# Row sums of the first half-batch by TensorE, and the weight rounding and the MLP's first block respaced, in a routed attention with an MLP behind it

## The chip, the cores and the metric

The kernel runs on one core of one Trainium2 chip. The metric is the device time of one execution in microseconds. The core's engines work side by side and wait for one another by semaphores: TensorE (PE in the profile; PEld is its weight load) does matrix products and transposes into PSUM, VectorE (DVE) and GpSimd (POOL) work element by element, ScalarE (ACT) does functions and copies, and SyncE (SP) issues the transfers. Each engine takes its instructions in the order of the program.

## What is computed

Attention over 4 batches, 8 heads, 768 positions and 64 dimensions, in which a query sees only the keys that have the same nearest centroid (16 per head), and then an MLP with a gated activation on the 3072 x 512 result. Cut from the reference:

```python
q_assign = np.argmax(np.einsum('bhsd,hcd->bhsc', q_n, c_n), axis=-1)
k_assign = np.argmax(np.einsum('bhsd,hcd->bhsc', k_n, c_n), axis=-1)
mask = q_assign[:, :, :, None] == k_assign[:, :, None, :]
scores = np.where(mask, scale * np.matmul(q, k.transpose(0, 1, 3, 2)), -1000000000.0)
attn = np.exp(scores - np.max(scores, axis=-1, keepdims=True))
attn = attn / (np.sum(attn, axis=-1, keepdims=True) + 1e-09)
x = np.matmul(attn, v)            # then (B,H,S,D) -> (B*S, H*D) = 3072 x 512
h = x @ w_in                      # 512 x 2048
g = h * (1.0 / (1.0 + np.exp(-1.702 * h)))
out = (g @ w_out).astype(np.float32)
```

The two weights come as 64-bit floats, and the kernel makes 32-bit ones of them itself.

## The kernel before

Heads go in pairs: 16 pairs (4 batches x 4), each in two halves of the queries, which gives 32 groups `g` of 6 units (one per 128 keys, `kt`). A batch is 8 groups: the first halves of its four pairs, then the second halves. A turn `t` handles two units, so a group takes TG = 3 turns, half a batch 12, a batch TB = 24, and the loop has 96 turns and two to finish. In the first batch (`p < HP`) the mask comes from a second matmul, `part`, added to the scores; later VectorE does it.

```python
xp = ctx.enter_context(tc.tile_pool(name="xp", bufs=HP + 2))    # HP = 4
ps_s = ... bufs=2; ps_o = ... bufs=1; ps_m = ... bufs=3          # PSUM; bank() takes of ps_m

def split_w(i):                     # first part of the rounding of weight chunk i of 32
    e = wp.tile([P, WN], I32, name="e")                          # wp: bufs=3, WN = 512
    nc.vector.tensor_scalar(out=e, in0=hi, ... bitwise_and)                       # L159
    nc.vector.tensor_scalar(out=w.bitcast(I32), in0=hi, ... bitwise_and)          # L161
    nc.scalar.activation(out=e, in_=e, func=AF.Relu, ...)                         # L163
    nc.scalar.activation(out=w, in_=w.bitcast(I32), func=AF.Copy, ...)            # L165

def join_w(i):
    nc.vector.scalar_tensor_tensor(out=e, in0=raw[:, :, 1], ..., in1=e, ...)      # L171
    nc.vector.scalar_tensor_tensor(out=w, in0=raw..., ..., in1=w, ...)            # L174
    nc.vector.tensor_tensor(out=w, in0=w, in1=e.bitcast(FP32), op=ALU.mult)       # L177

def round_next():                   # one round
    i = w_done[0]
    if i < NW:
        load_w(i + 2)
        split_w(i)
    if 0 < i <= NW:
        join_w(i - 1)
    w_done[0] += 1

def exps(u):                        # L409
    nc.scalar.activation(out=A_of[u] if p < HP else s, in_=s, func=AF.Exp, scale=SCALE)

def mask(u):
    ...                             # p >= HP: VectorE masks into A (L420)
    A = A_of[u]
    if kt == 0:
        return
    if kt == 1:
        sum_of[g] = ap.tile([P, 2, HALF], FP32, name="sum", bufs=2)
    nc.gpsimd.tensor_tensor(out=sum_of[g],                                        # L430
                            in0=A_of[u - 1] if kt == 1 else sum_of[g],
                            in1=A, op=ALU.add)

def values(u):
    for a in range(2):
        nc.tensor.matmul(out=o_of[g][a * D:(a + 1) * D, 0:HALF],                  # L441
                         lhsT=v_in[p][:, a, kt, :], rhs=A[:, a, :],
                         start=(kt == 0), stop=(kt == NJ - 1))
    ...                             # at kt == 5 ScalarE copies the result (L446)

def normalise(g):
    sm = sum_of.pop(g)
    ps = bank()
    for a in range(2):
        nc.tensor.matmul(out=ps[a * D:(a + 1) * D, 0:HALF], lhsT=ones,            # L453
                         rhs=sm[:, a, :], start=True, stop=True)
    rec = recs[g] = short()
    nc.vector.reciprocal(out=rec, in_=ps[:, 0:HALF])                              # L456
    nc.vector.tensor_tensor(out=x, in0=x, in1=rec, op=ALU.mult)                   # L458
    if g % HP == HP - 1:
        ffn.extend(ffn_chunks(g // HP))
```

`check` then has ScalarE test the reciprocals (L468, L470). The MLP of half a batch is 28 chunks: 16 `first(f)` (matmuls with `w_in`, L487; ScalarE's tanh, L492; VectorE's gate, L494) and 12 `second(n, part)` (matmuls with `w_out`, L504). Both begin with `round_to(...)`, which rounds the weights they need if that has not been done. Preparing a pair `p` takes seven steps `i`: transposes of q and k with a copy by ScalarE (0 to 3; L262, L267), products with the centroids (4, `prep_near`), the assignment by VectorE (5) and the spreading of the codes (6; in the first batch by transposes, L349, with copies by VectorE and ScalarE, L354, L356).

```python
rate = (NF + NH * (NF // 4)) / (TB / 2 - 0.5)
for t in range(NT + 2):
    ...                             # scores, part, exps of the turn's two units
    second = t >= TB // 2
    if second:
        round_next()
    ...                             # mask of the two units
    work = sorted(prep_at.get(t, ()), key=lambda w: PREP[w[1]] != prep_near)
    ...                             # prep_near steps; values of the turn before
    owed = owed + rate if ffn else 0.0
    g = (t - 2) // TG if t >= 2 and (t - 2) % TG == TG - 1 else None
    if g is not None and second:
        normalise(g)
    for p, i in work:
        prep(p, i)
    if g is not None and not second:
        normalise(g)
    if recs:
        check(*recs)
    if second or t and t % 4 != 3:
        round_next()
    while owed >= 1 and ffn:
        ffn.popleft()()
        owed -= 1
    if second and t % 2:
        round_next()
```

Of the kernel before, what the change touches and what calls it, by code (L numbers as in the profile page):

```python
# [10 lines left out]
I32 = mybir.dt.int32  # L11
# [27 lines left out]
def fast(  # L39
# [21 lines left out]
    nc = tc.nc  # L61

    B, H, S, D = q.shape
    NC = centroids.shape[1]
    DM, DF = moe_w_in.shape
    P = 128
    NJ = S // P
    HALF = S // 2
    NH = NJ // 2
    HP = H // 2  # L70
    NPAIR = B * HP
    NCH = DM // P
    NF = DF // P
# [10 lines left out]
    wp = ctx.enter_context(tc.tile_pool(name="wp", bufs=3))  # L84
    asg = ctx.enter_context(tc.tile_pool(name="asg", bufs=2))
    tmp = ctx.enter_context(tc.tile_pool(name="tmp", bufs=3))
    ap = ctx.enter_context(tc.tile_pool(name="ap", bufs=4))
    xp = ctx.enter_context(tc.tile_pool(name="xp", bufs=HP + 2))
    gp = ctx.enter_context(tc.tile_pool(name="gp", bufs=NF))
    yp = ctx.enter_context(tc.tile_pool(name="yp", bufs=2))  # L90
    dram = ctx.enter_context(tc.tile_pool(
        name="dram", bufs=2, space=bass.MemoryType.DRAM))
# [5 lines left out]
    def bank():  # L98
        return ps_m.tile([P, 512], FP32, name="m")
# [33 lines left out]
    WN = 512  # L133
# [6 lines left out]
    NW = len(w_chunks)  # L140
# [13 lines left out]
    def split_w(i):  # L154

        hi = w_raw[i][:, :, 1]
        w = w_chunks[i][0]
        e = wp.tile([P, WN], I32, name="e")
        nc.vector.tensor_scalar(out=e, in0=hi, scalar1=EXP, scalar2=None,  # L159
                                op0=ALU.bitwise_and)  # L160
        nc.vector.tensor_scalar(out=w.bitcast(I32), in0=hi, scalar1=0xFFFFF,  # L161
                                scalar2=None, op0=ALU.bitwise_and)
        nc.scalar.activation(out=e, in_=e, func=AF.Relu, scale=8.0,  # L163
                             bias=low[:, 0:1])
        nc.scalar.activation(out=w, in_=w.bitcast(I32), func=AF.Copy,  # L165
                             scale=2.0 ** -20, bias=1.0)
        w_pow[i] = e
# [12 lines left out]
    w_done = [0]  # L180

    def round_next():
# [4 lines that stand above are left out]
        if 0 < i <= NW:  # L187
            join_w(i - 1)
        w_done[0] += 1

    def round_to(n):
        while w_done[0] <= min(n, NW):
            round_next()

    load_qk(1, 0)
    load_v(0)
# [12 lines left out]
    ones = const.tile([P, D], FP32, name="ones")  # L209
# [34 lines left out]
    for a in range(2):  # L244
        rows = slice(a * D, (a + 1) * D)
        nc.vector.tensor_copy(
            out=cT[rows, :, a, :],
# [115 lines left out]
    PREP = [lambda p, i=i: prep_turn(p, i) for i in range(4)]  # L363
# [4 lines left out]

    NG = 2 * NPAIR
    NU = NG * NJ  # L370
    s_of, A_of, sum_of, o_of, O_of, xT_of = {}, {}, {}, {}, {}, {}

    def split(g):
        b, r = divmod(g, 2 * HP)
# [36 lines left out]

    def mask(u):

        g, kt = divmod(u, NJ)
        p, h = split(g)
        s = s_of.pop(u)
        if p >= HP:
            A_of[u] = ap.tile([P, 2, HALF], FP32, name="A")
            for a in range(2):
                nc.vector.scalar_tensor_tensor(  # L420
                    out=A_of[u][:, a, :],
                    in0=qcode[p][:, a, h * HALF:(h + 1) * HALF],
                    scalar=code[p][:, kt % NH, 1, kt // NH, a:a + 1],
                    in1=s[:, a, :], op0=ALU.is_equal, op1=ALU.mult)
        A = A_of[u]
        if kt == 0:
            return
        if kt == 1:
            sum_of[g] = ap.tile([P, 2, HALF], FP32, name="sum", bufs=2)
# [5 lines that stand above are left out]
        g, kt = divmod(u, NJ)  # L435
        p, h = split(g)
        if kt == 0:
            o_of[g] = ps_o.tile([P, 512], FP32, name="o")
        A = A_of.pop(u)
        for a in range(2):  # L440
            nc.tensor.matmul(out=o_of[g][a * D:(a + 1) * D, 0:HALF],  # L441
                             lhsT=v_in[p][:, a, kt, :], rhs=A[:, a, :],
                             start=(kt == 0), stop=(kt == NJ - 1))
        if kt == NJ - 1:
            O_of[g] = xp.tile([P, HALF], FP32, name="x")
            nc.scalar.copy(O_of[g], o_of.pop(g)[:, 0:HALF])  # L446

    def normalise(g):

        sm = sum_of.pop(g)  # L450
        ps = bank()
        for a in range(2):
            nc.tensor.matmul(out=ps[a * D:(a + 1) * D, 0:HALF], lhsT=ones,  # L453
                             rhs=sm[:, a, :], start=True, stop=True)
        rec = recs[g] = short()
        nc.vector.reciprocal(out=rec, in_=ps[:, 0:HALF])  # L456
        x = xT_of[g] = O_of.pop(g)
# [3 lines that stand above are left out]
# [11 lines left out]
                             accum_out=sums[:, 1, g:g + 1])  # L472


    ffn = deque()

    def ffn_chunks(bh):
        b, h = divmod(bh, 2)
        xT = [xT_of.pop(bh * HP + c) for c in range(NCH)]
        hs, ys = {}, {}  # L480

        def first(f):

            round_to((f * P // WN + 1) * NCH)
            ps = bank()
            for c in range(NCH):
                nc.tensor.matmul(out=ps[:, 0:HALF],  # L487
                                 lhsT=w_in[:, c, f * P:(f + 1) * P],
                                 rhs=xT[c], start=(c == 0),
                                 stop=(c == NCH - 1))  # L490
            g = hs[f] = gp.tile([P, HALF], FP32, name="g")
            nc.scalar.activation(out=g, in_=ps[:, 0:HALF], func=AF.Tanh,  # L492
                                 scale=0.851)
            nc.vector.scalar_tensor_tensor(out=g, in0=g, scalar=1.0,  # L494
                                           in1=ps[:, 0:HALF], op0=ALU.add,
                                           op1=ALU.mult)

        def second(n, part):
            round_to(NW // 2 + 4 * (part + 1))
            if part == 0:  # L500
                ys[n] = bank()
            ps = ys[n]
            for f in range(4 * part, 4 * part + 4):
                nc.tensor.matmul(out=ps[:, 0:DM],  # L504
                                 lhsT=hs[f][:, n * P:(n + 1) * P],
                                 rhs=w_out[:, f, :],
                                 start=(f == 0), stop=(f == NF - 1))
            if part == NF // 4 - 1:
                y = yp.tile([P, DM], FP32, name="y")
                nc.scalar.mul(y, ps[:, 0:DM], 0.5)  # L510
                nc.sync.dma_start(
                    out=out[b * S:(b + 1) * S, :].rearrange(
                        "(p j) n -> p j n", j=NJ)[:, h * NH + n, :], in_=y)

        return ([lambda f=f: first(f) for f in range(NF)]
                + [lambda n=n, part=part: second(n, part)
                   for n in range(NH) for part in range(NF // 4)])


# [25 lines left out]
        if i in (1, 3) and loads:  # L545
            load_qk(*loads.popleft())

    rate = (NF + NH * (NF // 4)) / (TB / 2 - 0.5)
    owed = 0.0
    for p, i in [(0, i) for i in range(6)] + [(1, i) for i in range(2)]:  # L550
        prep(p, i)
        if p == 0 and i in (1, 3):
# [1 line left out]
    for t in range(NT + 2):  # L554
        us = range(2 * t, 2 * t + 2) if t < NT else ()
        for u in us:
            scores(u)
        if t == 0:
            prep(0, 6)
        for u in us:  # L560
            part(u)
        for u in us:
            exps(u)
        second = t >= TB // 2
        if second:
            round_next()
        for u in us:
            mask(u)
        work = sorted(prep_at.get(t, ()), key=lambda w: PREP[w[1]] != prep_near)
        while work and PREP[work[0][1]] == prep_near:  # L570
            prep(*work.pop(0))
        if 1 <= t <= NT:
            for u in range(2 * t - 2, 2 * t):
                values(u)
        owed = owed + rate if ffn else 0.0
        g = (t - 2) // TG if t >= 2 and (t - 2) % TG == TG - 1 else None
        if g is not None and second:
            normalise(g)
        for p, i in work:
            prep(p, i)  # L580
        if g is not None and not second:
            normalise(g)
        if recs:
            check(*recs)
        if second or t and t % 4 != 3:
            round_next()
        while owed >= 1 and ffn:
            ffn.popleft()()
            owed -= 1
        if second and t % 2:  # L590
            round_next()
# [5 lines left out]
    ok1 = const.tile([P, 1], FP32, name="ok1")  # L597
    nc.vector.tensor_reduce(out=ok1, in_=ok, axis=AX.XY, op=ALU.min)
    for _ in range(NF // 2):
        ffn.popleft()()  # L600
    ps = bank()
    nc.tensor.transpose(out=ps[0:1, 0:P], in_=ok1, identity=ident)
    okt = const.tile([1, 1], FP32, name="okt")
# [2 lines left out]
    nc.vector.tensor_scalar(out=bad, in0=okt, scalar1=-1.0, scalar2=1.0,  # L606
                            op0=ALU.mult, op1=ALU.add)
    while ffn:
        ffn.popleft()()
        if len(ffn) == 4:  # L610
            is_bad = nc.values_load(bad[0:1, 0:1], min_val=0, max_val=1)
    return is_bad
# [440 lines left out]
```

## Time and profile before

| what | value |
|---|---|
| time, median of 3 runs | 1087.03 us (1086.46 to 1089.19) |
| span of the profiled run | 1087.3 us |
| TensorE busy | 1049.0 us, 96% |
| VectorE busy | 490.8 us, 45% |
| ScalarE busy | 354.8 us, 33% |
| GpSimd busy | 296.9 us, 27% (160 row-sum additions: 235.5 and 60.0 us) |
| mean granted TensorE clock | 0.99 |

Busy shares are means over a span with different stages; the windows by turn are needed to read them. A group of instructions is a line of the program with an engine and an operation: its count, its busy time, the mean duration of one in ns, and after the second bar the idle time of the engine just before them with what ended most of it. TensorE's records overlap one another, so its mean duration is longer than what a record adds to the time. In the timeline the brackets hold the engine's idle time before the row and what released it.

### The profile page before, as it was taken

What the parts mean: (1) busy time and instruction counts of PE and PEld (TensorE: products, weight loads), DVE (VectorE), ACT (ScalarE), POOL (GpSimd) and SP (SyncE); (2) the same over time, 40 slices, a digit from 0 to 9 for tenths busy, and PEclk for the clock granted to TensorE, in tenths of its full rate; (3) what the DMA queues carried; (4) which work ended last, traced back from release to release, by engine and by line L of the source; (5) the groups of instructions that cost most, each with busy time, mean ns of one, the idle gap of its engine ahead of it and who ended that gap; (6) DMA issues with size and microseconds to landing.
All of it is one profiled execution on the core that took longest, in us unless ns stands there. A gap on an engine that the chain in (4) does not pass through costs nothing. (4 is left out here: it accounts for less than half of the span.)

```text
span 1087.3 us, 10456 instructions
## 1 busy us (share of the span) xinstructions
PE 1049.0 (96%) x3982; PEld 492.6 (45%) x3982; DVE 490.8 (45%) x744; ACT 354.8 (33%) x665; POOL 296.9 (27%) x168
## 2 busy tenths in 40 slices
PE   7878799999999999999999999999999999999997
PEld 3423344445544455444454445444554445444543
DVE  3889999225442344424453164423552344431200
ACT  3755555223422333223432233223332133311100
POOL 2644223213232333123231142222332333230000
PEclk9998899999999999999999999999999999999999
DMA  7623443110100010002100000010000000000000
GB/s 199 165 81 116 131 133 111 46 49 17 49 23 27 10 30 15 31 25 54 51 23 17 15 20 15 15 48 32 8 7 12 10 10 1 1 10 20 1 11 22
DMA packets 64813, 45.13 MB, mean 42 GB/s; under 512 B 51953, under 2 KB 57585, under 8 KB 64753
## 3 DMA queue, kind: packets, MB, share of 16 engines
q1 hardware_dynamic: 64608, 44.33, 14.3%
q8 instruction: 33, 0.54, 0.2%
q14 instruction: 28, 0.22, 0.1%
q10 hardware_dynamic: 144, 0.03, 0.0%
HBM read 38.04 MB, written 6.31 MB: 41 GB/s over the span
## 5 line engine op out<-in xcount | busy, mean ns | idle before, releaser
L430 POOL TENSOR_TENSOR sum<-sum,A 128x768 f32<-128x768 f32 x128 | 235.5, 1840 | 461.3 <-DVE A L420 364.1
L487 PE MATMUL m<-x,w_in 128*128 128x384 f32 x1024 | 347.1, 494 | 9.7 <-ACT T L267 4.4
L504 PE MATMUL m<-w_out,g 128*128 128x512 f32 x768 | 337.8, 594 | 0.7 <-ACT short L282 0.7
L420 DVE SCALAR_TENSOR_TENSOR A<-qb,code,s 128x384 f32<-128x384 uint8 x288 | 157.6, 609 | 274.6 <-ACT s L409 251.9
L487 PEld LDWEIGHTS m<-x,w_in 128*128 128x128 f32 x1024 | 192.2, 192 | 149.1 <-issue 16.3
L504 PEld LDWEIGHTS m<-w_out,g 128*128 128x128 f32 x768 | 143.3, 190 | 175.6 <-issue 171.5
L494 DVE SCALAR_TENSOR_TENSOR g<-g,m 128x384 f32<-128x384 f32 x128 | 70.0, 553 | 220.4 <-ACT g L492 220.3
L384 PE MATMUL s<-T,T 64*128 64x384 f32 x768 | 152.9, 517 | 9.7 <-ACT A L409 9.6
L409 ACT ACTIVATE s<-s 128x768 f32<-128x768 f32 x144 | 107.9, 792 | 136.0 <-PE s L384 136.0
L441 PE MATMUL o<-A,inv 128*64 128x384 f32 x768 | 146.3, 502 | 0.0
L492 ACT ACTIVATE g<-m 128x384 f32<-128x384 f32 x128 | 61.7, 487 | 196.4 <-PE m L487 196.3
L430 POOL TENSOR_TENSOR sum<-A 128x768 f32<-128x768 f32 x32 | 60.0, 1876 | 215.6 <-DVE A L420 179.5
L384 PEld LDWEIGHTS s<-T,T 64*128 64x128 f32 x768 | 66.6, 189 | 94.6 <-issue 52.2
L456 DVE RECIPROCAL short<-m 128x384 f32<-128x384 f32 x32 | 81.6, 2551 | 25.8 <-PE m L453 25.8
L441 PEld LDWEIGHTS o<-A,inv 128*64 128x64 f32 x768 | 46.8, 137 | 84.8 <-issue 84.1
L510 ACT ACTIVATE y<-m 128x512 f32<-128x512 f32 x24 | 14.3, 595 | 155.8 <-PE m L504 142.7
L468 ACT ACTIVATE short<-short 128x384 f32<-128x384 f32 x32 | 16.7, 523 | 111.2 <-DVE x L458 111.2
L409 ACT ACTIVATE A<-s 128x768 f32<-128x768 f32 x48 | 36.1, 804 | 22.0 <-PE s L398 22.0
L267 ACT COPY T<-m 128x384 f32<-128x384 f32 x64 | 29.7, 480 | 37.2 <-PE m L262 37.1
L262 PE MATMUL m<-ident,in 128*128 128x128 f32 x192 | 33.9, 298 | 3.1 <-ACT T L267 1.7
L163 ACT ACTIVATE e<-e,low 128x512 int32<-128x512 int32 x32 | 23.1, 722 | 28.8 <-DVE e L159 28.8
L262 PEld LDWEIGHTS m<-ident,in 128*128 128x128 f32 x192 | 21.5, 146 | 22.4 <-issue 11.9
(68 smaller groups left out, 373.5 us busy)
## 6 DMA issues: line engine op xcount, KB each, us to landing
raw<-in_moe_w_in_dram SPq DMA_DIRECT2D x16, 512.0 KB
raw<-in_moe_w_out_dram SPq DMA_DIRECT2D x16, 512.0 KB
in<-in_q_dram SPq DMA_DIRECT2D x32, 192.0 KB
in<-in_k_dram SPq DMA_DIRECT2D x32, 192.0 KB
inv<-in_v_dram SPq DMA_DIRECT2D x16, 384.0 KB
out_dram<-y SPq DMA_DIRECT2D x24, 256.0 KB
qb<-line SPq DMA_DIRECT2D x12, 192.0 KB
line<-row SPq DMA_DIRECT2D x12, 1.5 KB
```

Of the source, the lines that this page charges most:

```text
L262: nc.tensor.transpose(out=ps[:, n * P:(n + 1) * P], in_=qk_in[p, w][:, h * NH + n].rearrange("p a d -> p (a d)"), identity=ident)
L267: nc.scalar.copy(dst, ps[:, 0:HALF])
L384: nc.tensor.matmul(out=ps[:, a, 0:HALF], lhsT=T[p, 1][rows, kt * P:(kt + 1) * P], rhs=T[p, 0][rows, h * HALF:(h + 1) * HALF], start=True, ...
L409: nc.scalar.activation(out=A_of[u] if p < HP else s, in_=s, func=AF.Exp, scale=SCALE)
L420: nc.vector.scalar_tensor_tensor(out=A_of[u][:, a, :], in0=qcode[p][:, a, h * HALF:(h + 1) * HALF], scalar=code[p][:, kt % NH, 1, kt // NH ...
L430: nc.gpsimd.tensor_tensor(out=sum_of[g], in0=A_of[u - 1] if kt == 1 else sum_of[g], in1=A, op=ALU.add)
L441: nc.tensor.matmul(out=o_of[g][a * D:(a + 1) * D, 0:HALF], lhsT=v_in[p][:, a, kt, :], rhs=A[:, a, :], start=(kt == 0), stop=(kt == NJ - 1))
L456: nc.vector.reciprocal(out=rec, in_=ps[:, 0:HALF])
L487: nc.tensor.matmul(out=ps[:, 0:HALF], lhsT=w_in[:, c, f * P:(f + 1) * P], rhs=xT[c], start=(c == 0), stop=(c == NCH - 1))
L492: nc.scalar.activation(out=g, in_=ps[:, 0:HALF], func=AF.Tanh, scale=0.851)
L494: nc.vector.scalar_tensor_tensor(out=g, in0=g, scalar=1.0, in1=ps[:, 0:HALF], op0=ALU.add, op1=ALU.mult)
L504: nc.tensor.matmul(out=ps[:, 0:DM], lhsT=hs[f][:, n * P:(n + 1) * P], rhs=w_out[:, f, :], start=(f == 0), stop=(f == NF - 1))
```

## The change

For the four groups of the first half-batch TensorE adds up the rows itself: beside each product with v it multiplies the same exponentials by ones, and accumulates over the six units in a PSUM bank of its own (`D_of`). GpSimd's additions of these groups go. Their normalisation can so come a turn earlier. In a turn with several preparations the transposes of the codes come last. The rounding of the weights starts in turn 0, goes on in every turn up to 11, and is then spread thinner, up to about turn 24. The MLP's chunks no longer force a rounding: a chunk waits until its weights are done. The MLP's first half-block is spread over 17 turns' worth of pace, so the following blocks run some three turns behind, for which `xp` gets one more buffer.

```diff
-    xp = ctx.enter_context(tc.tile_pool(name="xp", bufs=HP + 2))
+    xp = ctx.enter_context(tc.tile_pool(name="xp", bufs=2 * HP - 1))
...
-        e = wp.tile([P, WN], I32, name="e")
+        e = wp.tile([P, WN], I32, name="e", bufs=2)
...
-    def round_to(n):
-        while w_done[0] <= min(n, NW):
-            round_next()
...                                                          (mask)
-        if kt == 0:
+        if kt == 0 or g < HP:
             return
...                                                          (values)
+        if g < HP:
+            if kt == 0:
+                D_of[g] = bank()
+            for a in range(2):
+                nc.tensor.matmul(out=D_of[g][a * D:(a + 1) * D, 0:HALF],
+                                 lhsT=ones, rhs=A[:, a, :], start=(kt == 0),
+                                 stop=(kt == NJ - 1))
...                                                          (normalise)
+        if g < HP:
+            ps = D_of.pop(g)
+        else:
             ...                         (as before: bank(), L453)
...                                                          (first, second)
-            round_to((f * P // WN + 1) * NCH)
-            round_to(NW // 2 + 4 * (part + 1))
...
-        return ([lambda f=f: first(f) for f in range(NF)]
-                + [lambda n=n, part=part: second(n, part)
+        return ([((f * P // WN + 1) * NCH, lambda f=f: first(f))
+                 for f in range(NF)]
+                + [(NW // 2 + 4 * (part + 1),
+                    lambda n=n, part=part: second(n, part))
...                                                          (the loop)
-    rate = (NF + NH * (NF // 4)) / (TB / 2 - 0.5)
+    norm_at = {TG * g + (TG if g < HP else TG + 1): g for g in range(NG)}
+    owed, n_ffn = 0.0, NF + NH * (NF // 4)
...
-        if second:
+        if second or t == 0:
             round_next()
...
-        work = sorted(prep_at.get(t, ()), key=lambda w: PREP[w[1]] != prep_near)
+        work = sorted(prep_at.get(t, ()), key=lambda w: (
+            PREP[w[1]] != prep_near, w[0] < HP and w[1] == 6))
...
-        owed = owed + rate if ffn else 0.0
+        if not ffn:
+            owed = 0.0
+        else:
+            owed += n_ffn / (TB / 2 if t > TB else 17)
+        if t in norm_at and second:
+            normalise(norm_at[t])
...
-        if second or t and t % 4 != 3:
+        if not second:
             round_next()
-        while owed >= 1 and ffn:
-            ffn.popleft()()
+        while owed >= 1 and ffn and ffn[0][0] < w_done[0]:
+            ffn.popleft()[1]()
             owed -= 1
         if second and t % 2:
             round_next()
```

More of the change, by code (lines that the diff above doesn't have):

```diff
@@ L370, in fast @@
     NU = NG * NJ
-    s_of, A_of, sum_of, o_of, O_of, xT_of = {}, {}, {}, {}, {}, {}
+    s_of, A_of, sum_of, o_of, D_of, O_of, xT_of = {}, {}, {}, {}, {}, {}, {}
     def split(g):
@@ L448, in normalise @@
     def normalise(g):
[L450 to L454, printed above, removed]
+        if g < HP:
+            ps = D_of.pop(g)
+        else:
+            sm = sum_of.pop(g)
+            ps = bank()
+            for a in range(2):
+                nc.tensor.matmul(out=ps[a * D:(a + 1) * D, 0:HALF], lhsT=ones,
+                                 rhs=sm[:, a, :], start=True, stop=True)
         rec = recs[g] = short()
@@ L546, in prep @@
             load_qk(*loads.popleft())
-    rate = (NF + NH * (NF // 4)) / (TB / 2 - 0.5)
-    owed = 0.0
+    norm_at = {TG * g + (TG if g < HP else TG + 1): g for g in range(NG)}
+    owed, n_ffn = 0.0, NF + NH * (NF // 4)
     for p, i in [(0, i) for i in range(6)] + [(1, i) for i in range(2)]:
@@ L574, in fast @@
                 values(u)
-        owed = owed + rate if ffn else 0.0
-        g = (t - 2) // TG if t >= 2 and (t - 2) % TG == TG - 1 else None
-        if g is not None and second:
-            normalise(g)
+        if not ffn:
[4 more added lines that the diff above has]
+            normalise(norm_at[t])
         for p, i in work:
             prep(p, i)
-        if g is not None and not second:
-            normalise(g)
+        if t in norm_at and not second:
+            normalise(norm_at[t])
         if recs:
             check(*recs)
-        if second or t and t % 4 != 3:
+        if not second:
             round_next()
-        while owed >= 1 and ffn:
-            ffn.popleft()()
+        while owed >= 1 and ffn and ffn[0][0] < w_done[0]:
+            ffn.popleft()[1]()
             owed -= 1
@@ L599, in fast @@
     for _ in range(NF // 2):
-        ffn.popleft()()
+        ffn.popleft()[1]()
     ps = bank()
@@ L608, in fast @@
     while ffn:
-        ffn.popleft()()
+        ffn.popleft()[1]()
         if len(ffn) == 4:
```

## The prediction

> **What bounds the kernel now.** I read the page's table of forty slices first (TensorE at 9 from the eleventh slice on, 7 or 8 before), then cut the span by turns. A turn is two of the 192 attention units, and one exponential (L409) marks each unit, so the exponentials give the cuts: turns 0 to 11 (only attention) run from 16.2 to 85.6 us, turns 12 to 23 (the first MLP half-block joins) to 220.3. The table of windows:
>
> ```profile
> core 0: us, PE busy (x) PEld busy (x) DVE busy (x) ACT busy (x) POOL busy (x), PEclk, DMA share, GB/s
> ...
> 16.20:85.60 69.40, 58.61 (x369) 25.32 (x367) 51.89 (x71) 41.46 (x78) 38.23 (x20) 0.95 0.47 128
> 85.60:195.20 109.60, 98.13 (x391) 45.42 (x389) 103.37 (x146) 57.70 (x106) 32.96 (x17) 0.94 0.39 117
> 195.20:220.30 25.10, 24.76 (x87) 10.79 (x87) 3.12 (x2) 6.65 (x13) 7.24 (x4) 1.00 0.17 50
> 220.30:969.90 749.60, 746.89 (x2788) 351.66 (x2786) 311.95 (x478) 229.46 (x433) 213.44 (x118) 1.00 0.08 23
> 969.90:1087.30 117.40, 111.50 (x305) 54.12 (x301) 14.83 (x26) 14.14 (x28) 3.61 (x2) 0.99 0.03 12
> ```
>
> From 220 us on TensorE is busy all the time at full clock; what ends there is the sum of its work, and nothing the other engines do matters. Before 220 us it idles and its clock is throttled. From 85.6 to 195.2 VectorE is busy 103.4 of 109.6 us: there it is the bound, mostly with rounding the weights. So anything gained has to come from the first 220 us.
>
> How much is lost there? The groups of TensorE in the full stretch give what one record costs when nothing waits:
>
> ```profile
> L487 PE MATMUL m<-x,w_in 128*128 128x384 f32 x768 | 257.5, 489 | 0.3 <-ACT T L267 0.3
> L504 PE MATMUL m<-w_out,g 128*128 128x512 f32 x552 | 243.4, 595 | 0.0
> L384 PE MATMUL s<-T,T 64*128 64x384 f32 x570 | 111.4, 508 | 0.0
> L441 PE MATMUL o<-A,inv 128*64 128x384 f32 x568 | 107.3, 499 | 0.0
> L453 PE MATMUL m<-sum,ones 128*64 128x384 f32 x96 | 19.6, 486 | 0.0
> ```
>
> Busy time by count gives 0.335, 0.441, 0.195, 0.189 and 0.204 us. The mean duration of one is longer, because records overlap. The groups of different lines overlap a little too: all nine sum to 775.6 us against 746.9 busy, so I multiply sums by 0.963. With the counts of the same groups in the two early stretches (first: 96 of L384, 88 of L441, 50 of L398 at 0.128, 42 of L262 at 0.177, and small ones) the first twelve turns hold 57.7 us of work in 69.4 us: 11.7 lost. The next twelve hold 128 of L487, 64 of L504, 94 of L384, 96 of L441 and small ones, 117.1 us in 134.7: 17.6 lost. Together **29.3 us** is all that can be recovered there.
>
> Where does it go? First, VectorE and GpSimd hold each other up. In VectorE's timeline the same two instructions, once beside a running row sum and once without:
>
> ```profile
> 29.65 2.31 DVE L174 SCALAR_TENSOR_TENSOR w_in<-raw,w_in 128x512 f32<-128x512 uint32 x1
> 31.99 2.19 DVE L177 TENSOR_TENSOR w_in<-w_in,e 128x512 f32<-128x512 f32 x1
> ...
> 45.59 0.69 DVE L174 SCALAR_TENSOR_TENSOR w_in<-raw,w_in 128x512 f32<-128x512 uint32 x1
> 46.31 0.69 DVE L177 TENSOR_TENSOR w_in<-w_in,e 128x512 f32<-128x512 f32 x1
> ```
>
> Second, ScalarE takes its instructions in order, so its check and its share of the rounding, which wait for VectorE, stand ahead of the next exponentials, and those release TensorE's score buffers. ScalarE's timeline, and TensorE's right after:
>
> ```profile
> 44.43 0.52 ACT L468 ACTIVATE short<-short 128x384 f32<-128x384 f32 x1 [3.58 <-DVE x L458]
> ...
> 45.70 0.71 ACT L163 ACTIVATE e<-e,low 128x512 int32<-128x512 int32 x1
> ...
> 46.83 1.49 ACT L409 ACTIVATE A<-s 128x768 f32<-128x768 f32 x2
> ```
>
> ```profile
> 47.67 0.59 PE L384 MATMUL s<-T,T 64*128 64x384 f32 x2 [2.04 <-ACT A L409]
> ...
> 82.10 2.93 PE L384 MATMUL s<-T,T 64*128 64x384 f32 x8 [4.00 <-ACT A L409]
> ```
>
> ScalarE sat 3.58 us until the normalisation was done, and TensorE then 2.04 us until an exponential. At 82.10 it is the same wait, 4.00 us, and the eight score matmuls after it take 2.93 us, where other turns show 1.56.
>
> **What the Trainium skill says.** "SBUF — State Buffer", section "Who interferes with whom": a VectorE instruction with two SBUF inputs and a GpSimd instruction that reads SBUF exclude each other for the whole instruction. The trace agrees: 0.69 us alone, 2.2 to 2.3 beside a sum of 1.8 us. "TensorE: Matmul & The Clock Gate", section "What's actually happening": after about one idle window of 3.4 us the array gets half its clock. The trace agrees: from 81.3 to 85.6 us the granted clock is 0.52. The same page, section "The mechanism" (packing): matmuls that use different parts of the array run side by side. The trace agrees: a record of the 64-column L441 costs 0.189 us, one of the 128-column L487 with as many elements 0.335.
>
> **The change, part by part.**
>
> *Row sums on TensorE.* Groups 0 to 3 lose their 20 GpSimd additions and the 16 L453 records, and get 24 units x 4 records like those of L441: 96 x 0.189 - 16 x 0.204 = 14.9, times 0.963 = **+14.3 us** of TensorE work, certain. No other part adds or removes TensorE work; moving MLP chunks only moves it to where TensorE is full anyway. So the floor is 1087.0 + 14.3 - 29.3 = **1072 us**, with nothing lost in the first 24 turns; each microsecond still lost there adds one.
>
> *Rounding.* In turns 0 to 11 VectorE now does 8 rounds, with L174 at 1.30 and L177 at 1.25 us on average: 33.5 us of its 51.9. Without GpSimd a round takes 2.6 us from start to start (44.32 to 46.92 us), so the 13 rounds of after take 34 us: five more rounds for about nothing. TensorE's work in these turns grows from 57.7 to about 71 us, so VectorE, at some 52 us, is not the bound there. In turns 12 to 23 the 24 rounds cost 92.6 us (3.86 each, again beside sums). After, 18 rounds: 69.5, with 16 gates at 0.55 (8.8), four normalisations at 3.1 (12.4) and one assignment (2.3): 93 us. TensorE there: 117.1 less six deferred MLP chunks (24 chunks cost 68.5, 18 cost 48.1) plus the sums of turn 12: about 97 us. VectorE goes from the bound to 96% of it. The 17.6 us lost there should mostly go; I leave 4.
>
> *Order, and the normalisation a turn earlier.* In turns 3, 6 and 9 VectorE now does the assignment (2.6), the normalisation (3.1) and the split of a round (0.7) in a row, and ScalarE its check (1.3) and conversions (1.1), before the next exponentials: 8.8 us. TensorE can put the next turn's scores (1.9), values and sums (2.8) and transposes (at most 2) beside it, 6.7 us, if the three PSUM banks allow; one of them is now held by the sums. So 2 us is lost three times, up to 4 where the banks block: I take 6 in all, and 1 at the start. The later codes' transposes only keep other transposes from waiting behind them, and change little.
>
> *Second block three turns behind.* The first MLP half-block gets 1.65 chunks a turn for 12 turns, and about 8 of its 28 chunks come after turn 24. The tail grows by as many chunks; TensorE is full there, and the sum stays.
>
> The sum: 1087.0 + 14.3 - 29.3 + 6 + 1 + 4 = **1083 us**.
>
> **The rivals.** (1) *The stalls of the exponentials get longer.* The chain of 8.8 us is new, every turn now has a round (turns 3, 7 and 11 had none), and a bank is missing. For it: the gaps of 2.04 and 4.00 us are of this kind already. If 12 to 14 us stay lost in turns 0 to 11 as before, and 5 to 8 in the next twelve, 1089 to 1094. (2) *TensorE fills up almost wholly.* More work of its own lies beside each chain, and the throttled windows vanish with the long gaps: 2 to 4 us lost, 1074 to 1076. Against it: in-order waits of ScalarE remain. (3) *Loads.* Weight loads begin a turn earlier in the one queue that carries q, k and v; VectorE met a load only once in turns 12 to 23 (0.61 us). The DMA engines are busy 0.47 of turns 0 to 11, and five more loads of 512 KB in a longer stretch fit; if a transpose did wait, some 3 us.
>
> **Range and chances.** The floor is 1072; to reach "faster by over 2%" the time would have to be under 1065, below the floor, which only an error in the 29.3 could bring. "Slower by over 2%" needs 1109, 37 us lost where 29 are lost now. The first two rivals set the range, 1073 to 1094. Between the halves I lean a little to faster, since VectorE's relief is the largest term I can count, while the stalls are put together by hand. Faster over 2%: 0.03; within: 0.94; slower: 0.03.
>
> **What would show it.** Right: GpSimd with 140 additions instead of 160; L174 and L177 at 0.69 us in turns 0 to 11; that stretch longer than 69.4 us, near 78, and turns 12 to 23 near 102 instead of 134.7; TensorE full from then on. Wrong: gaps before L384 or L262 released by ScalarE of over 4 us in turns 4, 7 and 10, with a clock of 0.5 after them; or VectorE still busy over 95% in turns 12 to 23, and MLP matmuls waiting for its gates.

## The result and the profile after

The changed kernel takes **1106.41 us** (median; 1103.25 to 1107.63) against 1087.35 before: a ratio of 1.0169, with a 95% interval of 1.0144 to 1.0194. It is slower by 19 us, and 23 us over the predicted 1083.

The table of windows of the changed kernel, cut at the same turns as before (turns 0 to 11, turns 12 to 23, the rest of the loop, the tail):

```profile
core 0: us, PE busy (x) PEld busy (x) DVE busy (x) ACT busy (x) POOL busy (x), PEclk, DMA share, GB/s
...
15.70:102.70 87.00, 74.20 (x445) 33.11 (x443) 52.23 (x89) 48.02 (x87) 0.00 (x0) 0.90 0.45 126
102.70:215.30 112.60, 101.65 (x430) 47.42 (x430) 96.91 (x124) 55.91 (x105) 39.77 (x20) 0.94 0.35 105
...
967.40:1104.50 137.10, 131.20 (x353) 63.24 (x349) 15.65 (x28) 15.06 (x30) 3.62 (x2) 0.99 0.03 13
```

The first twelve turns grew from 69.4 to 87.0 us, the next twelve shrank from 134.7 to 112.6, and the tail grew from 117.4 to 137.1 because MLP chunks went there. Such shifts say little by themselves. What says something is the time lost: a window's length less the TensorE work in it, counted record by record with the prediction's costs times 0.963.

| kernel | span | TensorE work | lost in turns 0 to 11 | lost in turns 12 to 23 | lost elsewhere |
|---|---|---|---|---|---|
| before | 1087.3 | 1037.9 | 11.9 | 18.0 | 19.6 |
| after | 1104.5 | 1052.2 | 15.5 | 15.8 | 20.9 |

The span grew by 17.2 us. 14.3 of it are the row sums on TensorE. The time lost in the first 24 turns, 29.9 us before (29.3 in the prediction's count), is 31.3 after, where I had left 11 (6, 1 and 4).

The relief of VectorE came. Its groups in turns 0 to 11 of the changed kernel:

```profile
L177 DVE TENSOR_TENSOR w_in<-w_in,e 128x512 f32<-128x512 f32 x12 | 8.3, 692 | 0.4
L174 DVE SCALAR_TENSOR_TENSOR w_in<-raw,w_in 128x512 f32<-128x512 uint32 x12 | 8.2, 686 | 0.0
```

12 of each take 16.5 us; before, 8 of each took 20.4 there. VectorE is busy 52.2 of 87.0 us. But TensorE stands still. Its timeline in turns 4, 7, 10, 16 and 22, the five rows with a gap of over 3 us, and the two rows after the first of them:

```profile
48.31 0.90 PE L258 MATMUL m<-ident,in 128*128 128x128 f32 x3 [4.40 <-ACT T L263]
49.14 1.49 PE L345 MATMUL m<-ident_h,hot 128*64 128x128 bf16 x12
50.56 2.92 PE L380 MATMUL s<-T,T 64*128 64x384 f32 x8
...
73.29 0.49 PE L345 MATMUL m<-ident_h,hot 128*64 128x128 bf16 x6 [3.23 <-DVE qb L350]
...
94.75 2.93 PE L380 MATMUL s<-T,T 64*128 64x384 f32 x8 [3.97 <-ACT A L405]
...
139.54 5.49 PE L494 MATMUL m<-x,w_in 128*128 128x384 f32 x8 [3.54 <-ACT T L263]
...
196.35 7.27 PE L494 MATMUL m<-x,w_in 128*128 128x384 f32 x16 [5.45 <-ACT row L324]
```

All are turns with a normalisation or the turn after it. ScalarE's timeline over the first of them, from turn 3's copies to turn 4's exponentials:

```profile
37.01 0.48 ACT L450 COPY x<-o 128x384 f32<-128x384 f32 x1 [0.82 <-PE o L438]
44.01 0.52 ACT L475 ACTIVATE short<-short 128x384 f32<-128x384 f32 x1 [6.52 <-DVE x L465]
...
45.27 0.71 ACT L163 ACTIVATE e<-e,low 128x512 int32<-128x512 int32 x1
...
46.41 1.48 ACT L405 ACTIVATE A<-s 128x768 f32<-128x768 f32 x2
47.79 0.85 ACT L263 COPY T<-m 128x384 f32<-128x384 f32 x2
```

VectorE's timeline in the same stretch, from the first instruction of the assignment to the normalisation's last and the split behind it:

```profile
38.12 0.56 DVE L289 TENSOR_REDUCE best<-m 128x24 f32<-128x384 f32 x1 [3.01 <-PE m L283]
...
43.42 0.56 DVE L465 TENSOR_TENSOR x<-x,short 128x384 f32<-128x384 f32 x1
43.89 0.42 DVE L159 TENSOR_SCALAR e<-raw 128x512 int32<-128x512 int32 x1
```

ScalarE waits 6.52 us for VectorE's normalisation (L465). Then come the check (L475), the split's conversions (L163) and the exponentials (L405), and only then the copies (L263) that free the PSUM banks for TensorE's next transposes. Those start at 48.31, and at once.

Turns 16 and 22 have another start to the same wait. VectorE's timeline in turn 22:

```profile
191.63 1.91 DVE L159 TENSOR_SCALAR e<-raw 128x512 int32<-128x512 int32 x1
193.47 2.02 DVE L161 TENSOR_SCALAR w_out<-raw 128x512 int32<-128x512 int32 x1
...
197.34 2.55 DVE L463 RECIPROCAL short<-m 128x384 f32<-128x384 f32 x1
```

Beside it, GpSimd's sums and then ScalarE's timeline:

```profile
191.45 3.76 POOL L427 TENSOR_TENSOR sum<-sum,A 128x768 f32<-128x768 f32 x2 [5.71 <-ACT A L405]
```

```profile
193.58 0.72 ACT L163 ACTIVATE e<-e,low 128x512 int32<-128x512 int32 x1 [1.57 <-DVE e L159]
195.52 0.63 ACT L165 ACTIVATE w_out<-w_out 128x512 f32<-128x512 int32 x1 [1.22 <-DVE w_out L161]
196.06 0.24 ACT L324 CAST row<-m 12x128 uint8<-12x128 bf16 x1
```

A round whose two masks stand beside GpSimd's sums (1.91 and 2.02 us instead of 0.42 each) comes first, then the reciprocal. ScalarE has put the conversions that need the masks ahead of the copies, and TensorE waits 5.45 us.

### The profile page after: what moved, and what is told of

It is laid out like the page before. It is cut to its first block, busy times and chain, and to the rows that moved or that the text cites. A ratio compares the mean times of both kernels' runs of the same rounds, so it can differ in the third digit from the quotient of the medians.

```text
span 1104.5 us, 10602 instructions
## 1 busy us (share of the span) xinstructions
PE 1064.1 (96%) x4062; PEld 500.7 (45%) x4062; DVE 486.3 (44%) x744; ACT 355.6 (32%) x665; POOL 258.3 (23%) x148
## 5 line engine op out<-in xcount | busy, mean ns | idle before, releaser
L427 POOL TENSOR_TENSOR sum<-sum,A 128x768 f32<-128x768 f32 x112 | 205.1, 1831 | 434.8 <-DVE A L417 378.4
L405 ACT ACTIVATE s<-s 128x768 f32<-128x768 f32 x144 | 108.1, 794 | 164.9 <-PE s L380 161.2
L427 POOL TENSOR_TENSOR sum<-A 128x768 f32<-128x768 f32 x28 | 51.8, 1851 | 278.0 <-DVE A L417 163.4
L463 DVE RECIPROCAL short<-m 128x384 f32<-128x384 f32 x32 | 81.6, 2550 | 11.7 <-PE m L460 11.7
L475 ACT ACTIVATE short<-short 128x384 f32<-128x384 f32 x32 | 16.7, 523 | 117.8 <-DVE x L465 117.8
L263 ACT COPY T<-m 128x384 f32<-128x384 f32 x64 | 30.1, 479 | 43.1 <-PE m L258 43.1
L405 ACT ACTIVATE A<-s 128x768 f32<-128x768 f32 x48 | 36.1, 803 | 13.3 <-PE s L394 13.3
L163 ACT ACTIVATE e<-e,low 128x512 int32<-128x512 int32 x32 | 23.1, 722 | 20.7 <-DVE e L159 20.6
```

Source lines behind the costliest of these rows:

```text
L263: nc.scalar.copy(dst, ps[:, 0:HALF])
L427: nc.gpsimd.tensor_tensor(out=sum_of[g], in0=A_of[u - 1] if kt == 1 else sum_of[g], in1=A, op=ALU.add)
```

## The experiments

Theory D, written down after the first four runs: ScalarE takes its work in order, and what it does for VectorE (the check, the split of a round) stands ahead of the exponentials and copies on which TensorE depends; around a normalisation VectorE is late, so TensorE stops. The rivals: A, the added TensorE work is most of the loss; B, that work costs nothing; C, the PSUM bank held by the sums is missing; E, the collision of VectorE with GpSimd. The table has what each run left, the first two columns timed, the others from its profile, one execution (e3's is the slowest of its four, e4's the fastest).

| run | us | ratio to before (95%) | lost, turns 0 to 11 | lost, turns 12 to 23 |
|---|---|---|---|---|
| e1: GpSimd's sums, the rest as changed | 1098.12 | 1.0085 (1.0068 to 1.0102) | 17.8 | 19.2 |
| e2: before, with TensorE's sums | 1103.03 | 1.0126 (1.0109 to 1.0143) | 13.1 | 18.0 |
| e3: after, sums twice | 1113.84 | 1.0227 (1.0210 to 1.0244) | 11.5 | 12.2 |
| e4: after, check later | 1103.16 | 1.0130 (1.0110 to 1.0151) | 14.9 | 9.4 |
| e5: after, round first | 1103.24 | 1.0130 (1.0113 to 1.0147) | 14.7 | 13.5 |
| e6: after, both | 1093.87 | 1.0047 (1.0030 to 1.0063) | 7.7 | 9.8 |
| e7: before, check later | 1088.05 | 0.9996 (0.9987 to 1.0005) | 11.7 | 18.0 |
| e8: e1 with both | 1103.11 | 1.0139 (1.0120 to 1.0158) | 26.7 | 14.5 |
| e9: after, check later, rounds placed | 1079.34 | 0.9915 (0.9899 to 0.9932) | 2.2 | 1.2 |
| e10: after, rounds placed | 1092.53 | 1.0030 (1.0017 to 1.0044) | 10.9 | 6.5 |
| e11: e1 with a bank held | 1097.36 | 1.0070 (1.0048 to 1.0091) | 17.7 | 19.9 |
| e12: after, codes not last | 1106.10 | 1.0149 (1.0125 to 1.0174) | 18.0 | 14.1 |
| e13: e9 with GpSimd's sums | 1089.24 | 1.0005 (0.9997 to 1.0014) | 23.0 | 6.7 |
| e14: e9 with the old pace | 1088.12 | 1.0003 (0.9994 to 1.0012) | 2.0 | 5.0 |
| e9b: e9 again | 1079.15 | 0.9916 (0.9902 to 0.9931) | 0.6 | 1.2 |

### Which part costs what: e1, e2, e3

e1 takes TensorE's sums out of the changed kernel (all groups as before: GpSimd's additions, and the normalisation a turn later):

```diff
-        if kt == 0 or g < HP:
+        if kt == 0:
             return
-    norm_at = {TG * g + (TG if g < HP else TG + 1): g for g in range(NG)}
+    norm_at = {TG * g + TG + 1: g for g in range(NG)}
```

> The changed kernel with GpSimd's row sums back in all groups (normalisation of the first four groups a turn later, as before); rounding, order and pace as changed. Theory A (TensorE's 14.3 us of sums are paid in full, and the stalls at the normalisations are the rest): 14 us less TensorE work, but 13 rounds beside GpSimd's sums at 4.2 us instead of 2.6 would put 20 us more on VectorE in turns 0 to 11, part of it on the path: 1092 to 1100. Rival B (the sums lie in TensorE's idle time and cost nothing; the loss comes from the new order and pace): 1104 or more.

e2 puts the same part alone into the kernel before (the `D_of` matmuls, `normalise` and the turns of `norm_at` as in the change).

> The kernel before with one part of the change alone: row sums of the first four groups by TensorE and their normalisation a turn earlier; rounding and pace as before. Theory A: 14 us more TensorE work and a chain of assignment and normalisation in one turn, less the relief of VectorE: 1095 to 1103. Rival B: 1083 to 1088, the idle time takes it.

e3 issues the sums' matmuls twice, so the sums come out doubled; it measures a cost:

```diff
+            for again in range(2):
                 for a in range(2):
                     nc.tensor.matmul(out=D_of[g]..., lhsT=ones, rhs=A[:, a, :],
-                                 start=(kt == 0), stop=(kt == NJ - 1))
+                                 start=(kt == 0 and not again),
+                                 stop=(kt == NJ - 1 and again == 1))
```

> The changed kernel with each of the row-sum matmuls issued twice into the same bank (the sums come out doubled, so the output is halved; it measures a cost). 96 more records at 0.189 us times 0.963 are 17.5 us. Theory A: nearly all of it on the path, 1118 to 1124. Rival B: at most 1110, since it lies in idle time.

e1: 1098.12 us, as A had it, 8 less than the changed kernel. e2: 1103.03, at the upper end of A's range. B falls with both. But e1 is still 0.85% slower than before, with no work added to TensorE: the respacing alone loses 7 us more than before (17.8 + 19.2 against 11.9 + 18.0). And e3 refutes the simple form of A: of 17.5 us of added work only 7 arrive (1113.84 against 1106.41; 10 between the two profiles), under A's 1118 and over B's 1110, and 7.6 us less is lost (11.5 + 12.2 against 15.5 + 15.8). So part of such work lies in the stalls, and whatever removes the stalls will have to pay for the sums.

### What ScalarE stands behind: e4, e5, e6, e7, e8

"Check later" moves the check behind the next turn's exponentials:

```diff
         for u in us:
             exps(u)
+        if recs:
+            check(*recs)
...
-        if recs:
-            check(*recs)
...                                                          (after the loop)
+    check(*recs)
```

> The changed kernel with ScalarE's check of the reciprocals moved behind the next turn's exponentials. Theory A: the exponentials of turns 4, 7, 10, 17 and 23 no longer wait for the reciprocal and its check (1.4 us), but still for the split of the round behind it on VectorE, so the stalls get shorter by 1 to 2 us each: 1098 to 1103. Rival C (PSUM banks, one of them held by the sums, are what stops TensorE): 1105 to 1107.

"Round first" moves the round of turns 1 to 11 from the turn's end to just behind its exponentials:

```diff
-        if second or t == 0:
-            round_next()
+        round_next()
...
-        if not second:
+        if t == 0:
             round_next()
```

> The changed kernel with the round of turns 1 to 11 moved from the turn's end to just behind its exponentials. Theory D (ScalarE's order is what stops TensorE: the check and the split's two conversions stand ahead of the next exponentials, and both wait for VectorE's assignment and normalisation): with the split out of the way the exponentials of turns 4, 7 and 10 still wait for the check, so 1 us less each: 1102 to 1105. Rival C (PSUM banks): 1105 to 1108, since the copies that free banks now stand behind the split.

> Both moves on the changed kernel: round first, and the check behind the next turn's exponentials. Theory D: nothing that waits for the normalisation stands ahead of the exponentials of turns 4, 7 and 10; the three stalls of some 4 us fall to 2 or less and the half clock after them goes, about 10 us less in turns 0 to 11, on top of the 6 us that the later check took from turns 12 to 23: 1089 to 1096. Rival C: 1100 to 1103, no better than the later check alone.

e7 is the first diff on the kernel before, e8 both on e1.

> The kernel before with only the check moved behind the next turn's exponentials. Theory D: its gaps before scores in turns 5, 8, 10 and 11 (2.04, 1.25, 0.91, 4.00 us) are of this kind and shrink: 1080 to 1085. Rival: VectorE, busy 98% in turns 12 to 21, and the split behind the normalisation hold as before: 1086 to 1089.

> The respaced kernel with GpSimd's row sums (as e1) with both moves. Theory D: as e1 (1098) less 10 to 14 us of stalls: 1084 to 1089. Rival E (the collision of VectorE with GpSimd's sums is what makes the respaced rounding slow): 1094 to 1098.

Each move alone gains some 3 us (the interval of each ratio still overlaps that of the change), both together 12.5 (1093.87), as D had it, since the two waits stand one behind the other: with one gone the exponentials wait for the other. e4's timelines of ScalarE and TensorE have this at turn 4, with the split in the check's place:

```profile
37.51 0.48 ACT L450 COPY x<-o 128x384 f32<-128x384 f32 x1 [0.82 <-PE o L438]
44.85 0.72 ACT L163 ACTIVATE e<-e,low 128x512 int32<-128x512 int32 x1 [6.86 <-DVE e L159]
45.47 0.61 ACT L165 ACTIVATE w_in<-w_in 128x512 f32<-128x512 int32 x1
45.99 1.49 ACT L405 ACTIVATE A<-s 128x768 f32<-128x768 f32 x2
47.37 0.52 ACT L475 ACTIVATE short<-short 128x384 f32<-128x384 f32 x1
...
48.63 0.84 ACT L263 COPY T<-m 128x384 f32<-128x384 f32 x2
```

```profile
38.04 0.55 PE L283 MATMUL m<-ident,short 128*128 128x128 f32 x3
...
49.14 0.90 PE L258 MATMUL m<-ident,in 128*128 128x128 f32 x3 [4.73 <-ACT T L263]
```

From the end of TensorE's transposes for the assignment (38.59) the exponentials are 7.4 us away, instead of 8.3. But the check now stands between them and the copies, so TensorE's gap here is 4.73 us instead of 4.40; what e4 gains lies in turns 12 to 23. e7 is a miss for D's number and came as its rival had it: on the kernel before the later check is worth nothing (1088.05). Its gaps in turns 5 and 11 shrink by 0.9 us each, to 1.14 and 3.08, as the split behind the normalisation still holds the exponentials; turn 6 has a new gap of 1.70 us, and turns 12 to 23 lose 18.0 us as before. e8 misses both ranges: with GpSimd's sums the moves that won 12.5 us cost 5 (1103.11 against 1098.12), so there rival E points the right way, and its 1094 to 1098 was too low. One execution of e4 took 6188 us, over five times the others; I have not found why, and it is in no ratio.

e6 still loses 17.5 us, most of it in turns 4, 7, 16 and 22: TensorE's gaps there are 3.00, 2.92, 3.29 and 3.84 us, and copies of ScalarE behind a split end the first and the last two, as in the changed kernel.

### Rounds kept clear of the normalisations: e9, e10

```diff
-        if second or t == 0:
+        late = t in (16, 22)
+        if second and not late or t in (0, 3, 6, 9):
             round_next()
...
-        if not second:
+        if not second and t not in (3, 6, 9):
             round_next()
...
-        if second and t % 2:
+        if second and (t % 2 or late):
             round_next()
```

A round comes ahead of the assignment in turns 3, 6 and 9, at the end in the other turns up to 11, as in the changed kernel, and in turns 16 and 22 at the end instead of ahead of the reciprocal. e9 has this and the later check, e10 this alone.

> The changed kernel with the check behind the next turn's exponentials and the rounds kept clear of the normalisations: at the turn's start in turns 0, 3, 6 and 9, at its end in the other turns up to 11, and at the end instead of the start in turns 16 and 22. Theory D (in-order waits of ScalarE for VectorE around a normalisation): the gaps left with both moves before (3.00, 2.92, 3.29 and 3.84 us in turns 4, 7, 16 and 22, each released by a copy of ScalarE that stood behind the split) shrink to under 1 us, the half clock after them goes: 1094 less 10 to 14, so 1080 to 1085, faster than the kernel before. Rival (the waits only move to other turns): 1090 to 1095.

> The same placing of rounds with the check where the change has it. Theory D: turns 4, 7 and 10 still wait for the reciprocal and the check, 1 us less each; the stalls of turns 16 and 22 (3.54 and 5.45 us with half a clock after) mostly go: 1094 to 1099. Rival: 1102 to 1106.

e9 takes 1079.34 us, and e9b, the same kernel again, 1079.15, a ratio of **0.9916** (0.9902 to 0.9931): faster than both kernels, by only moving instructions, and just under D's 1080 to 1085. Its table of windows over the same two stretches:

```profile
15.70:89.10 73.40, 69.56 (x447) 30.61 (x443) 52.56 (x89) 48.07 (x88) 0.00 (x0) 0.98 0.51 145
89.10:187.40 98.30, 96.38 (x430) 45.37 (x430) 89.09 (x119) 56.44 (x105) 40.07 (x20) 1.00 0.38 118
```

TensorE does the same work as in the changed kernel, in 73.4 + 98.3 instead of 87.0 + 112.6 us. VectorE is as busy as there in the first stretch (52.6 us) and fuller in the second (89.1 of 98.3). Its load was not the bound. ScalarE's timeline from turn 3 to turn 4:

```profile
36.28 0.50 ACT L450 COPY x<-o 128x384 f32<-128x384 f32 x1
39.02 1.51 ACT L405 ACTIVATE A<-s 128x768 f32<-128x768 f32 x2 [2.24 <-PE s L394]
43.09 0.52 ACT L475 ACTIVATE short<-short 128x384 f32<-128x384 f32 x1 [2.55 <-DVE x L465]
```

The exponentials of turn 4 now wait for TensorE, and for nothing else. e10 has 1092.53 us (D: 1094 to 1099): without the later check half of it is won.

> The kernel of e9 again, for a narrower interval: 1078 to 1081, a ratio of 0.990 to 0.993.

### The bank and the order: e11, e12

e11 takes the bank that e1's normalisation needs two turns early and holds it (`if g < HP and kt == 2: D_of[g] = bank()` in `values`, and `ps = D_of.pop(g) if g < HP else bank()` in `normalise`).

> As e1 (GpSimd's sums in all groups, respaced), but the bank that the normalisation of the first four groups uses is taken two turns earlier and held, as TensorE's sums hold it, with no matmul added. Rival C (the missing PSUM bank stalls TensorE): e1's 1098 plus 4 to 8, so 1102 to 1106. Theory D: within 2 us of e1, 1096 to 1100.

e12 takes back the new order of preparations:

```diff
-        work = sorted(prep_at.get(t, ()), key=lambda w: (
-            PREP[w[1]] != prep_near, w[0] < HP and w[1] == 6))
+        work = sorted(prep_at.get(t, ()), key=lambda w: PREP[w[1]] != prep_near)
```

> The changed kernel without the new order of preparations: the codes' transposes come first in turns 4 and 7 again. Both theories: a small thing, 1104 to 1108. If the order matters for the banks (rival C), the copies of the codes would free their banks before ScalarE gets to the exponentials, or block it, and 3 to 5 us would show either way.

e11 has 1097.36 us beside e1's 1098.12: a bank held two turns costs nothing that can be measured there. In the changed kernel itself C was not tested alone, but e9 holds the same bank and loses 2.2 us in turns 0 to 11, so C falls as the cause. Banks are where TensorE stops, but because copies come late. e12 has 1106.10: the order is worth nothing.

### Do the sums and the pace pay without stalls: e13, e14

e13 is e9 with GpSimd's sums again, with rounds at the start in turns 0, 4, 7 and 10; e14 is e9 with the old pace (`owed += n_ffn / (TB / 2 - 0.5)` in every turn).

> The version of e9 (rounds placed clear of the normalisations, check later) with GpSimd's row sums in all groups again, normalised a turn later, and the rounds at the start in turns 0, 4, 7 and 10. It has 14 us less TensorE work than e9. Theory D with the collision: 13 rounds beside GpSimd's sums cost VectorE some 20 us more in turns 0 to 11, and the time lost there goes back to 20 to 29 us as in e1 and e8: 1090 to 1102, so TensorE's sums pay. Rival (without the stalls the sums are only extra work): 1066 to 1072.

> The version of e9 with the old pace of the MLP's chunks from the first half-block on (28 in 11.5 turns instead of 17). TensorE's work is the same and only moves. If the pace is what leaves VectorE room for the rounding, its gates now collide with the rounds, and chunks wait for weights: 1081 to 1087. If the pace is indifferent: 1078 to 1081.

Both pay. e13 takes 1089.24 us, just under the range of D with the collision: 14.3 us less work, and 10 us slower than e9, with the one placement of rounds that was tried, since 23.0 us are lost in turns 0 to 11. VectorE's groups there, two of the five instructions of a round:

```profile
L161 DVE TENSOR_SCALAR w_in<-raw 128x512 int32<-128x512 int32 x12 | 13.1, 1091 | 0.0
L159 DVE TENSOR_SCALAR e<-raw 128x512 int32<-128x512 int32 x12 | 11.8, 985 | 2.4 <-DMA raw<-in_moe_w_in_dram 2.2
```

They take 24.9 us, where the changed kernel, free of GpSimd there, has 10.1. e14 takes 1088.12, 9 more than e9 and above both my ranges. TensorE's timeline shows where:

```profile
201.94 2.90 PE L380 MATMUL s<-T,T 64*128 64x384 f32 x7 [7.54 <-DVE A L417]
...
208.91 31.07 PE L510 MATMUL m<-w_out,g 128*128 128x512 f32 x72
```

At the old pace the chunks overtake the rounding and are held back; at turn 24 TensorE has nothing to put beside VectorE's rounds and masks and idles 7.54 us, and then come nine chunks in a row.

## Why the prediction was wrong

*The sums' cost* was right. The 14.3 us in the table repeat the prediction's own costs, as the count uses them; what measures them, net of the relief for VectorE, is e2, which has this part alone and is 14.4 us over the kernel before (1103.03 against 1088.67, timed together). That they lie on the path is shown by e1 and e2, with the limit that e3 sets: where TensorE stalls, some of it is free.

*The rounding's cost* was right in turns 0 to 11: L174 and L177 at 0.69 us, VectorE busy 52.2 us for the foretold 52. In turns 12 to 23 it is busy 96.9 us, for 93.

*The step that failed in turns 12 to 23* is "The 17.6 us lost there should mostly go; I leave 4." 15.8 stayed. I took VectorE's busy share for the thing that loses time. e9 loses 1.2 us with VectorE busy 91% of these turns; the changed kernel loses 15.8 with 86%. What loses it is the order: with the later check alone 9.4 us are lost (e4), with the rounds moved behind the reciprocal in turns 16 and 22 alone 6.5 (e10), with both 1.2.

*The step that failed in turns 0 to 11* is "So 2 us is lost three times, up to 4 where the banks block: I take 6 in all, and 1 at the start." The chain itself was right: 8.8 us foretold, 8.3 from the end of the transposes (38.1) to the exponentials (46.41). What I put beside it, 6.7 us of other work, was too much: the last transposes and the codes need banks that ScalarE's copies free, and these come only behind the exponentials. TensorE stopped at 43.9, after 5.8 us, and could go on 1.9 us after the exponentials had begun, at 48.31: 8.3 + 1.9 - 5.8 is the 4.40 of turn 4. Turns 7 and 10 had 3.23 and 3.97 us. And I left out what I had shown myself of the kernel before, the clock after a gap: 0.54, 0.64 and 0.58 in turns 4, 7 and 10, the eight score matmuls at 2.9 us instead of 1.56. 15.5 us lost, where I had 7.

*The rivals.* The first named the mechanism; the sign of over 4 us behind ScalarE came in turn 4 (4.40) and nearly in turn 10 (3.97), with the clock at half, while VectorE in turns 12 to 23 was not over 95% busy; its 1089 to 1094 was too mild by 1.5 us in the first stretch (15.5 for 14) and 8 in the second (15.8 for 8). The second, TensorE filling up almost wholly (1074 to 1076), needs other placements: e9 is 3 us over it. No run reached the floor of 1072, but the change has a gain in it: e9 has all its parts, and lacks most of the waits.

*The sum*, again with the two terms as measured: 1087.0 + 14.3 - 29.9 + 15.5 + 15.8 = 1103, and 1 us more lost elsewhere, against the span of 1104.5.

*Gap and clock.* How much of the stalls is the wait and how much the slower clock after it? e9b has the changed kernel's records at a clock of 1.00, over the same two stretches:

```profile
17.60:89.40 71.80, 67.96 (x445) 30.09 (x443) 52.17 (x89) 47.95 (x88) 0.00 (x0) 1.00 0.49 141
89.40:187.70 98.30, 96.37 (x430) 45.36 (x430) 89.37 (x119) 56.37 (x105) 38.91 (x20) 1.00 0.38 118
```

TensorE stands idle in them for 3.8 and 1.9 us, in the changed kernel for 12.8 and 10.9: 18 us more of waiting. The same records keep it busy 6.2 and 5.3 us longer there, beside a clock of 0.90 and 0.94, so some 11.5 us are, by this estimate, the clock. The first line also shows what the count of lost time is worth: it puts 71.2 us of work where TensorE was busy for 67.96, so what is lost in turns 0 to 11 is some 3 us more than the tables say, and differences of under 2 us between kernels are not to be read, as e9 and e9b, one kernel, differ by 1.6.

Left open: whether e9's placement, made for a few turns by hand, is the best.

## What to carry to other kernels

When an engine takes its work in order, look at what stands between two of its instructions that the bound engine needs: work it does for a third engine there makes that engine's delays the bound engine's, however idle both are. Two such waits in a row must go together; taking away one shows little (3 us each in e4 and e5, against 12.5 for both), and its result would have led to the wrong verdict. And price a stall from where the bound engine really runs out of work, buffers included, with the clock it has afterwards.

## What the runs showed of the hardware

The array's clock can fall to half after shorter pauses than I had thought, and the same pause does not always bring it. In e9's turn 4 the one gap was 1.87 us, and TensorE was busy 1.57 of the 3.6 us around it; the granted clock of the next 3.4 us was 0.55:

```profile
42.40:46.00 3.60, 1.57 (x13) 1.06 (x14) 0.67 (x2) 2.55 (x7) 0.00 (x0) 1.00 0.41 91
46.00:49.40 3.40, 3.40 (x16) 1.61 (x17) 3.33 (x7) 1.94 (x3) 0.00 (x0) 0.55 0.58 151
49.40:52.80 3.40, 3.40 (x21) 1.22 (x18) 3.09 (x7) 1.51 (x2) 0.00 (x0) 0.95 0.45 146
```

e9b, the same kernel, has the same gap of 1.87 us in the same turn and as much work around it, and its clock stayed at 1.00:

```profile
44.30:47.90 3.60, 1.60 (x14) 1.09 (x15) 0.69 (x2) 2.54 (x7) 0.00 (x0) 1.00 0.27 63
47.90:51.30 3.40, 3.40 (x26) 1.65 (x27) 3.33 (x7) 2.93 (x5) 0.00 (x0) 1.00 0.67 179
```

So a stretch that is half empty can be enough, and need not be. A longer gap can pass too: with the one of 3.54 us in turn 16 the changed kernel has a clock of 0.75 over the 13.6 us from 133.5 on, and e12, with the same gap, 1.00 over the 13.6 us from 136.5 on. What decides is not shown here.

And VectorE's masks with one input (L159, L161), which I had counted at their mean, can be held by GpSimd's sums about as long as the additions with two: 0.42 us alone, 1.9 to 2.0 beside one.
